# Logits groups inside gate/up jobs, PV behind the up half, and another order of loads in a fused attention and gated-MLP kernel

## The chip, the cores and the metric

The kernel runs on one core of a Trainium2 chip. The metric is device time in microseconds for one execution. The kernel was run three times before the change; the median is what the change is compared with. The core has five engines that run side by side, each with a strict program order of its own: TensorE (PE: matmuls and their weight loads), VectorE (DVE), ScalarE (ACT), GpSimd (POOL) and SyncE (SP), which here mostly issues transfers (DMA). An engine waits when an instruction at the head of its order needs something that another engine or a transfer hasn't finished.

## What is computed

One block of a transformer with adaptive layer norm on 2048 rows of 448 columns. `c` and `w_mod` give six modulation vectors (sa, ca, ga, sb, cb, gb). The attention half works in four segments of 512 rows with 16 heads of 28 columns: causal softmax attention inside a segment, mixed by a gate with a read-out of a memory `M` that sums what earlier segments left. The second half is a gated MLP with 1792 hidden columns. Cut to what matters:

```python
h = layernorm(x) * (1 + ca) + sa
q, k, v = h @ wq, h @ wk, h @ wv            # 16 heads, 4 segments of 512
for s in range(4):
    logits = einsum('bhqd,bhkd->bhqk', qs, ks) * scale + mask
    a_dot = softmax(logits) @ vs
    pq = phi(qs)                            # t + 1 where t > 0, else exp(t)
    a_mem = (pq @ M) / (pq @ z + 1e-6)
    outs.append(g * a_mem + (1 - g) * a_dot)
    M = M + phi(ks).T @ vs;  z = z + phi(ks).sum()
x = x + ga * (concat(outs) @ wo)
h = layernorm(x) * (1 + cb) + sb
x = x + gb * ((sigmoid(h @ w_gate) * (h @ w_up)) @ w_down)
```

## The kernel before

The program is written as a schedule by hand. Attention runs over 4 segments, 4 head chunks `hc` of four heads, and 3 groups of logits per chunk. After each group, `run_fill` takes jobs (projections, output projection, gate/up, down) from a queue `fill` to keep TensorE busy, as many as `pace` allows by a nominal cost in ns. `later` puts small steps off to a nominal time; `tick` moves that time on; `need` forces what is still put off. All small PSUM results come from four buffers in rotation (`m_f32`, `m_bf16`); a logits group takes the other four banks.

```python
def logits(s, hc, g):
    ...
    lg = ps_lg.tile([P, 4, 512], F32, tag="lg", name="lg")
    ...
            for hs in range(4):
                r = slice(HP * hs, HP * hs + Dh)        # four row tiles of 32 rows, side by side
                nc.tensor.matmul(lg[:, hs, wid:wid + nq], lhsT=kT[r, hc, kb * P:(kb + 1) * P],
                                 rhs=qT[r, hc, kb * P:L], start=True, stop=True, tile_position=(HP * hs, 0))
    ...
    nc.scalar.activation(pT[:, :, w0:w0 + wid], lg[:, :, 0:wid], AF.Exp, scale=scale)
    ...

def pv(s, hc):
    ...                                                 # 40 matmuls into acc
    if s > 0:
        mem = m_f32("mem")
        ...                                             # 4 matmuls: memory read-out
    ...
    # r1 = 1/(acc sums), t1 = acc * r1, r2 = 1/(mem sums), t2 = mem * r2, ou = t1 + t2, all on VectorE

def gate_up(s, f0):
    h = hT_of[("2", s)]
    fcs = (f0, f0 + 1)
    ...
    for g, f in zip(gp, fs):
        for k in range(3):                              # 128 rows
            nc.tensor.matmul(g[:, 0:L], lhsT=wg_sb[:, k, f], rhs=h[:, k, :], start=(k == 0), stop=False)
    ...
    for g, u, f in zip(gp, up, fs):
        for dst, r, first in ((g, 0, False), (u, LW, True)):   # the last 64 rows: a pair of 64-row tiles
            nc.tensor.matmul(dst[:, 0:L], lhsT=wgu_sb[r:r + LW, f], rhs=h[r:r + LW, 3, :], start=first,
                             stop=not first, tile_position=(r, 0))
        tt = work.tile([P, L], F32, tag="tt", bufs=3)
        nc.scalar.activation(tt[:], g[:, 0:L], AF.Tanh, scale=0.5)
        tts.append(tt)
    for fc, u, f, tt in zip(fcs, up, fs, tts):
        for k in range(3):                              # 128 rows
            nc.tensor.matmul(u[:, 0:L], lhsT=wu_sb[:, k, f], rhs=h[:, k, :], start=False, stop=(k == 2))
        ...
        nc.vector.scalar_tensor_tensor(ft[:], tt[:], 1.0, u[:, 0:L], op0=ALU.add, op1=ALU.mult)
```

The layer norm of a later segment is spread in nominal time: statistics, `norm_t` with a DMA transpose on SyncE, and `modulate`, which waits for that transpose:

```python
            for t in range(TPS):
                later(5200 + 500 * t, lambda t=t: ln.norm(t) if by_pe else ln.norm_t(t), tag)
            if not by_pe:
                for kc in range(NK):
                    later(14500 + 500 * kc, lambda kc=kc: ln.modulate(kc, 0), tag)
```

The start of the program: `pad_copy` brings wq and wk from a staging buffer into their padded form.

```python
    for k in range(NK):
        pad_copy(nc.scalar, wq_sb, wq_st, k)
    for t in range(TPS):
        ln0.norm(t)
        if t == 1:
            for k in range(NK):
                pad_copy(nc.vector, wk_sb, wk_st, k)
            mod_evac(((0, 0), (1, 1)))
        for kc in range(NK):
            nc.tensor.transpose(pts[kc][:, t * P:(t + 1) * P], ln0.xn[:, t, kc * P:(kc + 1) * P], ident[:])
    for kc in range(NK):
        ln0.pe_evac(pts[kc], kc, 0)
```

And the main loop:

```python
            for g in range(3):
                if prev[0] >= 0 and g == 1:
                    pv(*prev)
                    tick(1100)
                logits(s, hc, g)
                tick(450)
                ...                                     # at s >= 1, hc == 1: queue wo, down, gate/up jobs
                debt = run_fill(pace[0] + debt)
                ...
                if prev[0] >= 0 and g == 2:
                    otr(*prev)                          # DMA transpose of ou to oT
```

`prep_b1` makes the replicated row ga, loads w_mod's fourth column block and scales wo; `prep_b3`, put between the first gate/up jobs, makes the row gb and scales wd in seven steps. w_mod passes through two buffers, `wm[j]` in buffer `j % 2`.

Of the kernel before, what the change touches and what calls it, by code (L numbers as in the profile page):

```python
# [13 lines left out]
P = 128  # L14
# [3 lines left out]
def kernel(  # L18
# [86 lines left out]

    load_x(nc.sync, 0, 2)
    load_x(nc.scalar, 2, 4)
    nc.sync.dma_start(c_col[:], c.rearrange("o (k p) -> p (o k)", p=KP))
# [37 lines left out]
    load_w(nc.sync, wq_st, A_wq)  # L146
    load_w(nc.scalar, wk_st, A_wk)
# [84 lines left out]
    def mod_rep(j, mul, name):  # L232
        rp = m_f32("rp")
        for k in range(NK):
            nc.tensor.matmul(rp[:, 0:D], lhsT=silu_bc[:, k, :], rhs=wm[j][:, k * D:(k + 1) * D],
                             start=(k == 0), stop=(k == NK - 1))
        rep = const.tile([P, D], BF16, name=name, tag="rep")
        nc.scalar.mul(rep[:], rp[:, 0:D], mul)
        return rep
# [61 lines left out]
    def ln1_start(s, by_pe=False):  # L301
        def start():
            ln = ln1_of[s] = LN([x_sb[:, s * TPS + t, :] for t in range(TPS)], ("1", s))
            tag = ("ln1", s)
            for t in range(TPS):
                later(900 * t, lambda t=t: ln.stats(t), tag)
            later(3600, lambda: ln.rstd(0, TPS), tag)
            for t in range(TPS):
                later(5200 + 500 * t, lambda t=t: ln.norm(t) if by_pe else ln.norm_t(t), tag)
            if not by_pe:  # L310
                for kc in range(NK):
                    later(14500 + 500 * kc, lambda kc=kc: ln.modulate(kc, 0), tag)
        return (0, start)
# [43 lines left out]
    def phi(src, wait, tag, then=None):  # L357
        e = work.tile([P, L], BF16, tag="e", bufs=6, name="e")
        nc.scalar.activation(e[:], src, AF.Exp)

        def fin():
            r = work.tile([P, L], BF16, tag="r", bufs=2, name="r")
            nc.vector.tensor_scalar(r[:], src, 0.0, 1.0, op0=ALU.max, op1=ALU.add)
            nc.vector.tensor_tensor(e[:], e[:], r[:], ALU.min)
            if then:
                then(e)
        later(wait, fin, tag)
        return e
# [30 lines left out]
    def logits(s, hc, g):  # L399
# [16 lines left out]
        if g == 0 and s > 0:  # L416
            pq_of[u] = phi(qT[:, hc, :], 4500, ("pq", u))
# [8 lines left out]
    def pv(s, hc):  # L426
# [12 lines left out]
        if s > 0:  # L439
            mem = m_f32("mem")  # L440
            memv = mem[:].rearrange("p (t h e) -> p t h e", h=4, e=HP)
            need(("pq", u), ("rm", s))
            pq = pq_of.pop(u)
            for qb in range(TPS):
                nc.tensor.matmul(memv[:, qb, :, 0:ME], lhsT=pq[:, qb * P:(qb + 1) * P], rhs=rm_of[s][:, hc, :, :],
                                 start=True, stop=True)
        ou = ou_bufs[(s * NHC + hc) % 2]
        ou_of[u] = ou
        cb = lambda i: coef[:, i:i + 1, hc * 4:(hc + 1) * 4].to_broadcast([P, TPS, 4])
        r1 = work.tile([P, TPS, 4], F32, tag="r1", bufs=2)  # L450
        nc.vector.tensor_tensor(r1[:], accv[:, :, :, Dh], cb(0), ALU.mult)
        nc.vector.reciprocal(r1[:], r1[:])

        def bc(r):
            return r[:].rearrange("p t (h o) -> p (t h) o", o=1).to_broadcast([P, TPS * 4, Dh])

        def num(a):
            return a[:].rearrange("p (th e) -> p th e", e=HP)[:, :, 0:Dh]

        ouv = ou[:].rearrange("p t h e -> p (t h) e")[:, :, 0:Dh]  # L460
# [4 lines left out]
        nc.vector.tensor_tensor(t1[:], num(acc), bc(r1), ALU.mult)  # L465
        r2 = work.tile([P, TPS, 4], F32, tag="r2", bufs=2)
        nc.vector.scalar_tensor_tensor(r2[:], memv[:, :, :, Dh], 1e-6, cb(1), op0=ALU.add, op1=ALU.mult)
        nc.vector.reciprocal(r2[:], r2[:])
        t2 = work.tile([P, TPS * 4, Dh], F32, tag="t2", bufs=1)
        nc.vector.tensor_tensor(t2[:], num(mem), bc(r2), ALU.mult)  # L470
        nc.vector.tensor_tensor(ouv, t1[:], t2[:], ALU.add)
# [29 lines left out]

    def gate_up(s, f0):
# [9 lines left out]
        for g, u, f in zip(gp, up, fs):  # L512
            for dst, r, first in ((g, 0, False), (u, LW, True)):
                nc.tensor.matmul(dst[:, 0:L], lhsT=wgu_sb[r:r + LW, f], rhs=h[r:r + LW, 3, :], start=first,  # L514
                                 stop=not first, tile_position=(r, 0))
            tt = work.tile([P, L], F32, tag="tt", bufs=3)
            nc.scalar.activation(tt[:], g[:, 0:L], AF.Tanh, scale=0.5)  # L517
            tts.append(tt)
        for fc, u, f, tt in zip(fcs, up, fs, tts):
# [36 lines left out]
    def gu_jobs(s):  # L556
        return [(GU, lambda fc=fc: gate_up(s, fc)) for fc in range(0, NFC, 2)]
# [6 lines left out]
    def run_fill(ns):  # L564
        while fill and ns > 0:
# [6 lines left out]
    def prep_b1():  # L572
        ga = mod_rep(2, 1.0, "ga")
        wm[4] = load_wm(nc.sync, 4)
        for k in range(0, NK, 2):
# [6 lines left out]
    def prep_b2():  # L582
        mod_cols(((3, 2), (4, 3)))
        wm[5] = load_wm(nc.sync, 5)

    def prep_b3():
        gb = mod_rep(5, 0.5, "gb")
        for fc in range(0, NFC, 2):
            later(1700 * fc + 800, lambda fc=fc: scale_w(wd_sb, fc, gb), "wd")
# [15 lines left out]
    for t in range(TPS):  # L605
# [3 lines left out]
        if t == 1:  # L609
            silu_ops()  # L610
# [3 lines left out]
    for k in range(NK):  # L614
        pad_copy(nc.scalar, wq_sb, wq_st, k)
    for t in range(TPS):
        ln0.norm(t)
        if t == 1:
            for k in range(NK):
                pad_copy(nc.vector, wk_sb, wk_st, k)  # L620
            mod_evac(((0, 0), (1, 1)))
        for kc in range(NK):
            nc.tensor.transpose(pts[kc][:, t * P:(t + 1) * P], ln0.xn[:, t, kc * P:(kc + 1) * P], ident[:])
    for kc in range(NK):
        ln0.pe_evac(pts[kc], kc, 0)
    load_x(nc.sync, TPS, 2 * TPS)
# [16 lines left out]
    def load_wm3():  # L643
        wm[3] = load_wm(nc.sync, 3)
# [11 lines left out]
    def spread(jobs, steps, every):  # L656
        steps, res = list(steps), []
        for i, j in enumerate(jobs):
            res.append(j)
            if i % every == every - 1 and steps:  # L660
# [4 lines left out]
    early_loads = [load_wo, lambda: load_x(nc.sync, 3 * TPS, 4 * TPS), load_wm3] \  # L665
        + [piece(wg_sb, B_w_gate, k) for k in range(NK)] + [piece(wu_sb, B_w_up, k) for k in range(NK)]
    fill.extend(sp(load_bw2))
    fill.extend(spread(j0[3:6] + sp(late_consts) + j0[6:10] + [ln1_start(2)] + j0[10:] + ln1_pe_jobs(1) + m[0][0:1]
                       + j1[:8], early_loads, 2))
    fill.extend([ln1_start(3)] + m[1][0:1] + j1[8:] + [(1000, prep_b1)])  # L670
    fill.extend(spread(j2[:4] + m[0][1:] + j2[4:8] + [(2000, prep_b2)], [piece_wd(f, min(f + 4, NFC)) for f in range(0, NFC, 4)], 2))
    fill.extend(j2[8:] + m[1][1:])
    fill.extend(j3)
# [7 lines left out]
    for s in range(NSEG):  # L681
        for hc in range(NHC):
            prev = (s, hc - 1) if hc else (s - 1, NHC - 1)
            for g in range(3):
                if prev[0] >= 0 and g == 1:
                    pv(*prev)
                    tick(1100)
                logits(s, hc, g)
                tick(450)
                if s >= 1 and hc == 1 and g == 0:  # L690
# [3 lines left out]
                    fill.clear()  # L694
                    for w in wo_jobs(s - 1):
                        fill.append(w)
                        if tail and s > 1:
                            fill.append(tail.pop(0))
# [4 lines left out]
                    else:  # L703
                        fill.extend(h2_jobs(s - 1) + gj[:1] + [(1000, prep_b3)] + m[2][0:1] + gj[1:5] + m[2][1:] + gj[5:])
# [8 lines left out]
    dj = down_jobs(last - 1)  # L713
    run_fill(2000)
    pv(last, NHC - 1)
    tick(1100)
    run_fill(6000)
    otr(last, NHC - 1)
    fill.extend(dj[:2])
    run_fill(3000)  # L720
# [3 lines left out]
    fill.extend(dj[2:])  # L724
# [33 lines left out]
```

The softmax here doesn't subtract the row's maximum and nothing guards it: scores larger than these inputs give would overflow.

## Time and profile before

| what | value |
|---|---|
| device time, median of 3 runs | 274.89 us (274.32 to 276.37) |
| span of the profiled execution | 275.1 us |
| instructions | 5225 |
| mean granted TensorE clock | 0.975 |
| HBM read and written | 10.67 MB, 1.84 MB |

Some of the groups of instructions in that profile, with what their engine waited for before them:

| line, engine, what | count | busy us, mean ns | idle before, most of it ended by |
|---|---|---|---|
| L415 ScalarE exp of logits | 48 | 76.6, 1595 | 55.1, PE logits |
| L524 VectorE product of gate and up | 56 | 36.8, 684 | 36.7, PE up |
| L517 ScalarE tanh of the gate | 56 | 30.3, 595 | 44.9, PE gate |
| L530 PE down | 224 | 43.7, 353 | 0.0 |
| L509 PE gate, full array | 155 | 40.4, 380 | 1.0, VectorE |
| L521 PE up, full array | 164 | 40.2, 381 | 0.5 |
| L412 PE logits (four forms) | 256 | 17.7, 310 | 3.4, ScalarE exp |
| L437 PE PV | 640 | 19.0, 177 | 1.4, GpSimd mask |

A line number is that of the kernel before. Busy time of an engine counts its instructions from start to end; matmuls overlap, so a mean duration of 380 ns goes with a start every 216 ns. "Idle before" is what the engine stood still just ahead of such an instruction, and the name is that of the engine whose result ended the wait. A row of tenths shows one digit for each of 40 equal slices of the span; the clock row is the share of full clock that TensorE was granted. L274, L374 and L477 are the DMA transposes that SyncE issues (hT, pk, oT); L278 is `modulate`; L342 brings kT out of PSUM.

### The profile page before, as it was taken

To read this page: it belongs to the slowest core of one execution; us is meant where nothing else is said; L and a number is where in the kernel's file an instruction comes from. 1 tells how busy PE (TensorE), PEld (TensorE's weight loads), DVE (VectorE), ACT (ScalarE), POOL (GpSimd) and SP (SyncE) were. 2 spreads that over 40 slices of the span, in tenths; PEclk is the share of its full clock that TensorE was granted. 3 is DMA by queue.
4 is the path that set the end of the run, shared out by engine and by line. 5 is a ranking of instruction groups with operands and counts; after the bars stand their busy time and mean duration, and the time that the engine had idled before them with its cause. 6 is when DMAs were issued, how large, how long until landed. Compare 5 with 4: busy or idle time off the path is not lost.

```text
span 275.1 us, 5225 instructions
## 1 busy us (share of the span) xinstructions
PE 246.6 (90%) x2029; PEld 114.7 (42%) x2054; DVE 185.0 (67%) x429; ACT 139.2 (51%) x171; POOL 69.6 (25%) x130
## 2 busy tenths in 40 slices
PE   7599798896788689889989989999999999999995
PEld 2344444553343334444344443535443445433352
DVE  4569799944378748897995665797774669434421
ACT  1268489774727578666622767653564220033300
POOL 4109421450424312114351222224220004000000
PEclk9979799997979999999999999999999999999999
DMA  5999539488911100220031100003120001400001
GB/s 144 263 235 284 113 64 221 70 147 142 245 40 39 42 19 0 60 57 21 19 76 35 38 19 21 1 21 84 28 55 20 21 0 42 94 9 0 0 26 43
DMA packets 40960, 19.66 MB, mean 71 GB/s; under 512 B 29672, under 2 KB 40040, under 8 KB 40936
## 3 DMA queue, kind: packets, MB, share of 16 engines
q1 hardware_dynamic: 39720, 18.30, 30.8%
q10 hardware_dynamic: 1216, 1.03, 1.4%
q8 instruction: 16, 0.26, 0.5%
q14 instruction: 8, 0.07, 0.1%
HBM read 10.67 MB, written 1.84 MB: 45 GB/s over the span
## 4 chain that ended last, share of the span: by engine, by line
PE 44%; DVE 20%; DMA 6%; ACT 3%; issue 3%; SPq 1%; POOL 1%; DVEq 0%; ACTq 0%
PE ups L521 12%; PE dps L530 11%; PE gps L509 10%; PE gps L514 4%; DMA hT<-xn 3%; DVE st L257 3%; PE lg L412 2%; DVE x_sb L489 2%; PE acc L437 2%; DVE fT L524 2%; ACT pT L415 2%; DMA oT<-ou 2%; PE pwo L486 2%; DMA pk<-e 2%; DVE t L470 1%
## 5 line engine op out<-in xcount | busy, mean ns | idle before, releaser
L415 ACT ACTIVATE pT<-lg 128x2048 bf16<-128x2048 f32 (+1 forms) x48 | 76.6, 1595 | 55.1 <-PE lg L412 55.0
L524 DVE SCALAR_TENSOR_TENSOR fT<-tt,ups 128x512 bf16<-128x512 f32 x56 | 36.8, 684 | 36.7 <-PE ups L521 28.5
L423 POOL TENSOR_SCALAR_AFFINE_SELECT pT<-pT 128x512 bf16<-128x512 bf16 x64 | 41.2, 662 | 67.7 <-ACT pT L415 67.7
L517 ACT ACTIVATE tt<-gps 128x512 f32<-128x512 f32 x56 | 30.3, 595 | 44.9 <-PE gps L514 44.9
L530 PE MATMUL dps<-wd_sb,fT 128*128 128x448 bf16 x224 | 43.7, 353 | 0.0
L509 PE MATMUL gps<-hT,wg_sb 128*128 128x512 bf16 x155 | 40.4, 380 | 1.0 <-DVE t L465 0.4
L521 PE MATMUL ups<-hT,wu_sb 128*128 128x512 bf16 x164 | 40.2, 381 | 0.5 <-issue 0.5
L530 PEld LDWEIGHTS <-fT 128*128 128x128 bf16 x224 | 21.5, 98 | 20.5 <-issue 0.6
L521 PEld LDWEIGHTS <-wu_sb 128*128 128x128 bf16 x168 | 14.1, 98 | 25.5 <-issue 12.3
L261 POOL TENSOR_SCALAR rs<-mv 128x1 f32<-128x1 f32 (+2 forms) x21 | 5.2, 248 | 75.9 <-DVE mv L258 75.9
L509 PEld LDWEIGHTS <-wg_sb 128*128 128x128 bf16 x168 | 15.2, 98 | 20.0 <-issue 2.7
L437 PEld LDWEIGHTS <-pT 128*128 128x128 bf16 x640 | 18.8, 97 | 5.9 <-issue 2.2
L337 PE MATMUL pq<-hT,wq_sb 128*128 128x512 bf16 x60 | 18.2, 406 | 3.2 <-DVE hT L296 1.9
L257 DVE BATCH_NORM_STATS2 st<-x_sb 128x6 f32<-128x448 bf16 x32 | 19.8, 617 | 1.8 <-DMA x_sb<-in_A_x_dram 1.3
L412 PE MATMUL lg<-qT,kT 28*128 28x512 bf16 (+3 forms) x256 | 17.7, 310 | 3.4 <-ACT pT L415 3.4
L437 PE MATMUL acc<-vt,pT 128*128 128x29 bf16 x640 | 19.0, 177 | 1.4 <-POOL pT L423 1.2
L514 PE MATMUL ups<-hT,wgu_sb 64*128 64x512 bf16 x56 | 18.0, 382 | 2.0 <-DVE t L470 1.1
L534 DVE TENSOR_TENSOR ot<-dps,x_sb 128x448 bf16<-128x448 f32 x16 | 9.8, 618 | 13.2 <-PE dps L530 10.7
L514 PE MATMUL gps<-hT,wgu_sb 64*128 64x512 bf16 x56 | 17.1, 381 | 1.6 <-DVE hT L278 1.3
L349 PE MATMUL pv<-wv_sb,hT 128*128 128x448 bf16 x64 | 14.6, 367 | 4.2 <-DVE kT L342 4.2
L337 PE MATMUL pq<-hT,wk_sb 128*128 128x512 bf16 x61 | 17.0, 394 | 1.0 <-ACT qT L340 0.7
L486 PE MATMUL pwo<-wo_sb,oT 128*128 128x448 bf16 x64 | 14.8, 366 | 2.2 <-DMA oT<-ou 2.1
(88 smaller groups left out, 261.9 us busy)
## 6 DMA issues: line engine op xcount, KB each, us to landing
wm<-in_w_mod_dram SPq DMA_DIRECT2D x5, 392.0 KB, 7.9
out_dram<-ot SPq DMA_DIRECT2D x16, 112.0 KB, 1.7
x_sb<-in_A_x_dram SPq DMA_DIRECT2D x3, 448.0 KB, 7.3
wg_sb<-in_B_w_gate_dram SPq DMA_DIRECT2D x3, 448.0 KB, 9.1
wu_sb<-in_B_w_up_dram SPq DMA_DIRECT2D x3, 448.0 KB, 3.9
wd_sb<-in_B_w_down_dram SPq DMA_DIRECT2D x3, 448.0 KB, 3.7
wm<-in_w_mod_dram ACTq DMA_DIRECT2D x1, 392.0 KB
wo_sb<-in_A_wo_dram SPq DMA_DIRECT2D x4, 98.0 KB
```

Source lines behind the costliest of these rows:

```text
L257: nc.vector.bn_stats(st[:], self.srcs[i])
L337: nc.tensor.matmul(pq[:, 0:L], lhsT=head_cols(w_sb, k, hc), rhs=h[:, k, :], start=(k == 0), stop=(k == NK - 1))
L412: nc.tensor.matmul(lg[:, hs, wid:wid + nq], lhsT=kT[r, hc, kb * P:(kb + 1) * P], rhs=qT[r, hc, kb * P:L], start=True, stop=True, tile_posi ...
L415: nc.scalar.activation(pT[:, :, w0:w0 + wid], lg[:, :, 0:wid], AF.Exp, scale=scale)
L423: nc.gpsimd.affine_select(out=blk, in_=blk, compare_op=ALU.is_ge, fill=0.0, base=0, pattern=[[0, 4], [1, P]], channel_multiplier=-1)
L437: nc.tensor.matmul(accv[:, qb, hs, 0:ME], lhsT=pT[:, hs, c0:c0 + P], rhs=vt[:, kb, hc * 4 + hs, 0:ME], start=(kb == 0), stop=(kb == qb))
L509: nc.tensor.matmul(g[:, 0:L], lhsT=wg_sb[:, k, f], rhs=h[:, k, :], start=(k == 0), stop=False)
L514: nc.tensor.matmul(dst[:, 0:L], lhsT=wgu_sb[r:r + LW, f], rhs=h[r:r + LW, 3, :], start=first, stop=not first, tile_position=(r, 0))
L517: nc.scalar.activation(tt[:], g[:, 0:L], AF.Tanh, scale=0.5)
L521: nc.tensor.matmul(u[:, 0:L], lhsT=wu_sb[:, k, f], rhs=h[:, k, :], start=False, stop=(k == 2))
L524: nc.vector.scalar_tensor_tensor(ft[:], tt[:], 1.0, u[:, 0:L], op0=ALU.add, op1=ALU.mult)
L530: nc.tensor.matmul(dp[:, 0:D], lhsT=fT_of[(s, fc)][:, t * P:(t + 1) * P], rhs=wd_sb[:, fc, :], start=(fc == 0), stop=(fc == NFC - 1))
```

## The change

Some changes are of order only; no matmul is added or taken away.

- A gate/up job is split: the full-array gate matmuls and the 64-row tile pairs are a first job, the full-array up matmuls a second. `run_fill` stops behind a first half where it can, the next logits group comes right behind the tile pairs, and the up half follows it.
- PV of the chunk before comes behind that up half instead of ahead of the logits group.
- The memory read-out becomes a step of its own one group earlier (group 0 instead of 1), with t2 in two buffers.
- gb is made in `prep_b1`, and wd is scaled from there on instead of between the gate/up jobs; for that w_mod's blocks 3 and 5 change places in the order of loads, ga and gb get a buffer each, and wd is loaded before gate and up weights.
- At the start, c is loaded first on ScalarE's queue, wq and wk are each split over both queues, the norms and transposes of segment 0 come ahead of the copies, and the copies of wq are shared by ScalarE and VectorE.
- Segments 2 and 3 start their first norm at other places in the queue and modulate at other nominal times; the tail is queued in another way, and phi's buffers go from six to five.

```diff
+    nc.scalar.dma_start(c_col[:], c.rearrange("o (k p) -> p (o k)", p=KP))
     load_x(nc.sync, 0, 2)
     load_x(nc.scalar, 2, 4)
-    nc.sync.dma_start(c_col[:], c.rearrange("o (k p) -> p (o k)", p=KP))
...
-    load_w(nc.sync, wq_st, A_wq)
-    load_w(nc.scalar, wk_st, A_wk)
+    for st, w in ((wq_st, A_wq), (wk_st, A_wk)):
+        nc.sync.dma_start(st[:, 0:2, :], w[0:2 * P, :].rearrange("(k p) n -> p k n", p=P))
+        nc.scalar.dma_start(st[:, 2, :], w[2 * P:3 * P, :])
+        nc.scalar.dma_start(st[0:LW, 3, :], w[3 * P:D, :])
...
-                    later(14500 + 500 * kc, lambda kc=kc: ln.modulate(kc, 0), tag)
+                    later(mod_at + 500 * kc, lambda kc=kc: ln.modulate(kc, 0), tag)
...
-            pq_of[u] = phi(qT[:, hc, :], 4500, ("pq", u))
+            pq_of[u] = phi(qT[:, hc, :], 3600, ("pq", u))
...
+    def mem_read(s, hc):
+        u = (s, hc)
+        mem = m_f32("mem")
...
+        t2 = work.tile([P, TPS * 4, Dh], F32, tag="t2", bufs=2)
+        t2_of[u] = t2
         nc.vector.tensor_tensor(t2[:], num(mem), bc(r2), ALU.mult)
...
+        half[0] = (s, fcs, up, fs, tts)
+
+    def gate_up2():
+        s, fcs, up, fs, tts = half.pop(0)
+        h = hT_of[("2", s)]
         for fc, u, f, tt in zip(fcs, up, fs, tts):
...
-        return [(GU, lambda fc=fc: gate_up(s, fc)) for fc in range(0, NFC, 2)]
+            jobs += [(GU - 6 * MM, lambda fc=fc: gate_up(s, fc)), (6 * MM, gate_up2)]
...
-        while fill and ns > 0:
+        while fill and (ns > 0 or fn is gate_up2 and fill[0][0] == GU - 6 * MM):
...
     def prep_b1():
         ga = mod_rep(2, 1.0, "ga")
         wm[4] = load_wm(nc.sync, 4)
+        gb = mod_rep(5, 0.5, "gb")
+        wm[3] = load_wm(nc.sync, 3)
+        for fc in range(0, NFC, 2):
+            later(8000 + 2000 * fc, lambda fc=fc: scale_w(wd_sb, fc, gb), "wd")
...
-    for k in range(NK):
-        pad_copy(nc.scalar, wq_sb, wq_st, k)
     for t in range(TPS):
         ln0.norm(t)
         if t == 1:
-            for k in range(NK):
-                pad_copy(nc.vector, wk_sb, wk_st, k)
             mod_evac(((0, 0), (1, 1)))
...
+    for k in range(2):
+        pad_copy(nc.scalar, wq_sb, wq_st, k)
+        pad_copy(nc.vector, wq_sb, wq_st, 2 + k)
     for kc in range(NK):
         ln0.pe_evac(pts[kc], kc, 0)
+    for k in range(NK):
+        pad_copy(nc.vector, wk_sb, wk_st, k)
...
-    fill.extend([ln1_start(3)] + m[1][0:1] + j1[8:] + [(1000, prep_b1)])
...
+    fill.extend(j1[8:9] + [ln1_start(3, mod_at=19000)] + m[1][0:1] + j1[9:] + [(1800, prep_b1)])
+    fill.extend(spread(j2[:4] + m[0][1:] + j2[4:8] + [(2000, prep_b2)], early_loads[11:], 2))
+    fill.extend(j2[8:] + j3[:2] + m[1][1:] + j3[2:])
...
             for g in range(3):
+                logits(s, hc, g)
+                tick(450)
+                if fill and fill[0][1] is gate_up2:
+                    fill.popleft()[1]()
+                    tick(6 * MM)
+                    debt -= 6 * MM
+                if prev[0] > 0 and g == 0:
+                    mem_read(*prev)
+                    tick(250)
                 if prev[0] >= 0 and g == 1:
                     pv(*prev)
-                    tick(1100)
-                logits(s, hc, g)
-                tick(450)
+                    tick(1000)
...
-    run_fill(6000)
+    run_fill(1500)
     otr(last, NHC - 1)
-    fill.extend(dj[:2])
-    run_fill(3000)
+    run_fill(3500)
     for c, fn in wo_jobs(last):
         fn()
         tick(c)
-    fill.extend(dj[2:])
+    fill.extend(dj)
```

## The prediction, made before the changed kernel was run

> **What bounds the kernel now.** I read the page first (busy shares, the 40 slices), then the busy time by stage, then what TensorE (PE) waited for, then the chain that ended last. From the page:
>
> ```profile
> PE 246.6 (90%) x2029; PEld 114.7 (42%) x2054; DVE 185.0 (67%) x429; ACT 139.2 (51%) x171; POOL 69.6 (25%) x130
> PEclk9979799997979999999999999999999999999999
> ```
>
> TensorE is the bound, but not evenly, and its granted clock dips to 0.7 in four slices, all before 84 us. Busy time by stage (columns: stretch, length, then busy us and instructions for PE, weight loads, VectorE (DVE), ScalarE, GpSimd; then clock, DMA share, GB/s):
>
> ```profile
> 0.00:77.00 77.00, 63.00 (x563) 30.97 (x571) 51.51 (x137) 48.67 (x62) 27.32 (x53) 0.93 0.81 174
> 77.00:132.00 55.00, 47.66 (x466) 22.19 (x473) 44.14 (x105) 35.50 (x42) 16.08 (x28) 0.97 0.15 33
> 132.00:224.00 92.00, 88.51 (x764) 40.58 (x773) 65.19 (x142) 47.42 (x54) 22.94 (x41) 1.00 0.14 33
> 224.00:275.10 51.10, 47.39 (x240) 20.98 (x241) 24.15 (x48) 7.63 (x15) 3.31 (x8) 1.00 0.12 29
> ```
>
> PE idles 14.0 us in the first stage, 7.3 in the second, 3.5 in the third and 3.7 in the last, most of that after its last matmul. So the open money lies before 132 us; after it only fewer or cheaper PE steps help. PE's waits, longest in total (us, times, longest):
>
> ```profile
> PE pv L349 <- DVE kT L342: 4.2, 2, 2.8
> PE lg L412 <- ACT pT L415: 3.4, 6, 1.1
> PE cp L218 <- DMA wm<-in_w_mod_dram: 2.2, 1, 2.2
> PE pwo L486 <- DMA oT<-ou: 2.1, 1, 2.1
> PE pq L337 <- DVE hT L296: 1.9, 2, 1.6
> ```
>
> The largest is a wait for VectorE, and VectorE was itself waiting: its own waits list `DVE hT L278 <- DMA hT<-xn` with one wait of 5.1 us. The chain between 58 and 80 us (start, us, what) shows it:
>
> ```profile
> 59.20 1.26 SPq L274
> ...
> 60.55 2.46 DMA hT<-xn
> ...
> 63.13 0.73 DVE hT L278 x2
> 63.87 0.60 DVE kT L342
> 64.47 0.61 DVE hT L278 x2
> 65.08 4.28 DMA pk<-e
> ...
> 71.31 5.57 DMA oT<-ou
> ```
>
> The modulation of segment 3's hT stands too early in VectorE's strict order. Its transposed input lands only at 63 us, the kT evacuation behind it is held, PSUM stays full and PE stops until 64.5. The steady state, PE's timeline:
>
> ```profile
> 158.50 0.29 PE L412 MATMUL lg<-qT,kT 28*128 28x256 bf16 x4
> 158.72 1.47 PE L509 MATMUL gps<-hT,wg_sb 128*128 128x512 bf16 x6
> 160.12 0.39 PE L514 MATMUL gps<-hT,wgu_sb 64*128 64x512 bf16 x1
> ...
> 160.66 1.47 PE L521 MATMUL ups<-hT,wu_sb 128*128 128x512 bf16 x6
> 162.06 0.40 PE L412 MATMUL lg<-qT,kT 28*128 28x512 bf16 x4
> 162.39 1.17 PE L437 MATMUL acc<-vt,pT 128*128 128x29 bf16 x40
> ```
>
> Start to start, six full matmuls take 1.40 us before the tile pairs. The two pairs 160.12 and 160.35 are 0.23 apart, and the full matmuls follow 0.31 after the second pair. Plain spacing is 0.216 (the chain has six gps matmuls in 1.29 us from 241.80), so six should take 1.30: each passage between a full-array matmul and a row-tiled one costs about 0.10 us. The same shows at logits: 0.33 from 162.06 to the next full matmul, for one 512-wide step.
>
> **What the skill says.** The Trainium skill, "TensorEngine Tiling (Array Packing)", section "Tiling Modes" (Key Properties), says that changing the tiling mode, not merely the tile, drains TensorE. The 0.10 us agrees with a drain at 128-to-64, 64-to-128 and 128-to-32 rows; no matmul pair in this trace goes from 64 to 32 directly, so whether that passage costs the same isn't shown. "TensorE: Matmul & The Clock Gate", Part 1, says an idle window of about 3.4 us puts the clock to half. The trace agrees in effect, after waits of even 2.8 us: four pv matmuls from 64.52 took 1.65 us against 0.93 for four at 23.43, and the stretch 60 to 68 us has a clock of 0.79. "DMA: Bandwidth & Descriptors", section "Issuing engines are not separate DMA queues", says that loads issued from two engines run on the same 16 DMA engines and interleave. So the split of wq and wk brings order (wq whole before wk), not bandwidth. Here they landed nearly together: VectorE's wk copies began at 11.87 us and ScalarE's wq copies at 12.34, and DMA was 0.93 busy over the first 20 us.
>
> **The change part by part.**
>
> *Start.* Before, VectorE holds the last two norms behind the wk copies (DMA wait of 2.4 us to 11.87), so the transposes end about 14.1; ScalarE does four wq copies (2.0 us) before its two hT evacuations (14.27 to 15.72). The first q matmul starts at 14.77. After, the norms go first, so transposes can end about 12.5, right after the modulation columns (wm lands 10.54, columns out about 11.6). The wq copies are two of 0.56 us on ScalarE beside two of about 0.27 on VectorE (the means of such copies before), and wk's come after the evacuations. If wq lands about 11.5, the first q matmul can start near 13.2. Minus 1.5 us; the c vector first on its queue also frees silu, which held VectorE until 7.4.
>
> *Segment 2 and 3 normalisation.* Segment 2's starts two jobs (1.5 us) earlier with modulation 0.5 us closer: it meets the two hT waits of PE at 47 to 49 us (0.23 + 0.68): minus 0.9. For segment 3 the modulation moves from 14.5 to 19 us after a start that is one job later. The 2.8 us stall goes, and with it the half-clock work after it (4 pv matmuls 1.65 for 0.93, PV, logits and dM some 0.5 more): gross about 4. Against it, hT, pk and oT transposes still queue behind one another on SyncE, which issues one per 1.2 us, and the new second wm load sits among them. I keep half: minus 2.
>
> *oT wait.* PV of (0,3) ran late because of that stall, and its transpose took 5.57 us behind three wd loads. It should come some 3 us earlier, and two segment-3 projections now stand ahead of dM. Minus 1 of the 2.1 us wait.
>
> *wd scaling.* Seven VectorE multiplies of 0.63 us (4.4 us) leave 100 to 128 us, where VectorE is 90% busy (12.64 of 14 us between 104 and 118) and is the chain, for roughly 52 to 80 us, where it has room before 77. PE idles 4.8 us between 95 and 132. The memory read-out one group ahead takes r2, its reciprocal and t2 (1.0 us) out of the burst after PV, and its PSUM buffer is released earlier (waits of PE on t L470: 1.1 us in all). Together minus 3.0: 2.5 in that stretch and 0.5 before it.
>
> *Logits behind tile pairs.* Walking the fill queue with the job costs in the code, 14 of the 48 logits groups come directly behind a gate half and ahead of its up half. There 128-64-128 plus 128-32-128 (four passages) becomes 128-64-32-128 (three): 14 x 0.10 = minus 1.4. The tanh now precedes the exp on ScalarE, so up results no longer wait behind a 1.88 us exp (VectorE waited 8.2 us for tt): minus 0.7 of the 2.9 us that PE waits between 132 and 224.
>
> *PV later, the tail, the rest.* PV (40 matmuls, 1.0 us) only moves. In the tail the same queue walk gives the same order of gate, wo and down jobs as before; zero. The matmul count is unchanged.
>
> Sum: 1.5 + 0.9 + 2 + 1 + 3.0 + 1.4 + 0.7 = 10.5 us, giving 264.4. I do not take it all. PE is one in-order engine fed by transposes whose pace is set elsewhere, so an early gain can be waited away at the next landing: I strike 3 of the 5.4 us won before 77 us, which leaves **267.4**.
>
> **Rivals.** (a) *The transpose queue is the bound until 77 us.* The segment-1 pk transposes need the buffer that dM of segment 0 frees at 53.4, and everything on SyncE stands behind them; DMA share is 0.81. Then the removed kT stall becomes a wait at dM or pwo, and only the later parts count (5.1 us): about 270. For it: the chain passes from hT to pk to oT without PE. Against it: PV, which starts the last oT, was itself late through the stall. (b) *A new wait for w_mod.* Both remaining wm loads (392 KB each) are now issued after the second replicated row, near 53 us, and the modulation columns of the second norm need both; they ran at 58.5, with the one load issued at 54.65. If the second lands 2 us late PE stalls there, about 269.5. (c) *PSUM.* Between gate half and up half all four small buffers are held; if PV or read-out then makes the next gate half wait for fT, 14 jobs at 0.2 us give back 3 us: about 270. The order (read-out and PV after the up half) speaks against it. (d) *64 to 32 costs double*: then the name-giving part brings nothing, 268.8.
>
> **Range and chances.** The parts are independent enough that one rival at a time is likely: 267 to 270; several together, 272 to 273. If early gains carry through, 263. The 2% line is 269.4, two microseconds above my figure, so I give faster 0.62, same 0.34. A loss over 2% needs new waits larger than all the gains; nothing points there: 0.04.
>
> **What would show it.** Right: first q matmul near 13.2; no 2.8 us PE wait on kT and no VectorE wait of 5 us on hT; fewer clock dips between 60 and 84; no wd multiply after 100 us; logits starting about 0.10 behind a 64-row pair's last matmul with the up half 0.10 behind them; PE busy above 92% of the span. Wrong: a long PE wait on wm, pk or oT before 77 us; tile-to-tile gaps of 0.2 us; waits on fT or acc at gate halves; or a start no earlier because wq still lands at 12.3.

## The result and the profile after

The changed kernel took 267.94 us (median of 4 runs, 267.26 to 268.67), the kernel before beside it 275.63. The ratio is 0.9726 (95% interval 0.967 to 0.9782); on another chip, with more runs, it was 0.9748 (0.9718 to 0.9778). The prediction was 267.4.

The sum was close; how it came about was not all as predicted. From the page after (the same two lines as of before):

```profile
PE 241.1 (91%) x2030; PEld 113.3 (43%) x2054; DVE 183.4 (69%) x431; ACT 137.8 (52%) x169; POOL 70.8 (27%) x130
PEclk9999999988999999999999999999999999999999
```

The four dips of the clock to 0.7 are gone, two to 0.8 are left. Busy time by stage, cut at the same times as before:

```profile
0.00:77.00 77.00, 64.97 (x627) 31.93 (x635) 58.19 (x155) 49.81 (x62) 28.51 (x57) 0.98 0.78 174
77.00:132.00 55.00, 49.58 (x494) 23.81 (x498) 45.73 (x109) 38.17 (x45) 20.21 (x35) 1.00 0.17 37
132.00:224.00 92.00, 88.57 (x722) 41.24 (x728) 64.03 (x142) 42.21 (x50) 22.10 (x40) 1.00 0.14 33
224.00:275.10 51.10, 37.99 (x193) 16.36 (x193) 15.50 (x28) 7.60 (x14) 0.01 (x1) 0.99 0.09 24
```

In the first 77 us TensorE (PE) is busy for 2.0 us more and starts 64 more matmuls: the clock, not only idle time, was won there. PE's waits after (us in total, times, longest; in this kernel L339 are the q and k projections, L351 v, L387 the memory sum dM, L494 the output projection, L220 the modulation columns, and L344 brings kT out of PSUM):

```profile
PE lg L414 <- ACT pT L417: 2.8, 5, 0.8
PE pq L339 <- DVE hT L298: 2.8, 2, 2.3
PE pv L351 <- DVE kT L344: 2.0, 2, 1.1
PE pwo L494 <- DMA oT<-ou: 1.9, 1, 1.9
PE dM L387 <- DMA pk<-e: 1.6, 1, 1.6
PE ups L524 <- DVE x_sb L497: 1.5, 2, 0.8
PE warm L613 <- POOL ident L160: 1.4, 1, 1.4
PE cp L220 <- DVE silu L183: 1.2, 1, 1.2
PE cp L220 <- DMA wm<-in_w_mod_dram: 1.1, 1, 1.1
...
PE acc L439 <- ACT tt L527: 0.5, 1, 0.5
PE mem L463 <- ACT tt L527: 0.5, 1, 0.5
```

The 2.8 us stall on kT is gone. In its place stand waits for the landing of w_mod (1.1) and of pk (1.6), and the wait for oT is almost as long as it was (1.9 of 2.1; 1.4 in a second profile of this kernel). Two waits on tanh near the end are new: PV and read-out of the last chunk stand between a gate half and its up half.

Cut by what PE does instead of by time, the gain lies elsewhere than predicted. Starts in us from PE's timeline in each profile, of the first q matmul, the first dM, the first gate matmul, the first down matmul and the last segment's output projection, and the span:

| kernel | first q | first dM | first gate | first down | last wo | span |
|---|---|---|---|---|---|---|
| before | 14.77 | 52.38 | 93.45 | 135.80 | 224.36 | 275.1 |
| changed | 12.54 | 48.90 | 90.06 | 127.23 | 215.34 | 265.7 |
| difference, stage by stage | -2.2 | -1.2 | +0.1 | -5.2 | -0.5 | -0.4 |

The second replicated row (two rows' eight matmuls take 1.68 us, so 0.8 for one) moved from the fourth of these stages into the second; apart from it the second won 2.1 us and the fourth 4.3, and the third, where the stall was, nothing. The profiled execution of before was one of its longer ones (276.8 us), so the two traces differ by 9.4 us where the medians differ by 7.7.

### The profile page after: what moved, and what is told of

It reads as the page before. It is cut to its first block, busy times and chain, and to the rows that moved or that the text cites. A ratio compares the mean times of both kernels' runs of the same rounds, so it can differ in the third digit from the quotient of the medians.

```text
span 265.7 us, 5242 instructions
## 1 busy us (share of the span) xinstructions
PE 241.1 (91%) x2030; PEld 113.3 (43%) x2054; DVE 183.4 (69%) x431; ACT 137.8 (52%) x169; POOL 70.8 (27%) x130
## 4 chain that ended last, share of the span: by engine, by line
PE 43%; DVE 6%; ACT 2%; issue 2%; DMA 1%; POOL 0%; DVEq 0%
PE dps L545 14%; PE ups L536 10%; PE gps L519 9%; PE gps L524 4%; PE acc L439 2%; PE pwo L494 2%; DVE fT L539 1%; PE lg L414 1%; ACT pT L417 1%; DVE ot L549 1%; DMA hT<-xn 1%; ACT tt L527 1%; DVE t L451 1%; DVE hT L280 1%; PE mem L463 1%
## 5 line engine op out<-in xcount | busy, mean ns | idle before, releaser
L425 POOL TENSOR_SCALAR_AFFINE_SELECT pT<-pT 128x512 bf16<-128x512 bf16 x64 | 42.6, 681 | 68.9 <-ACT pT L417 68.9
L519 PE MATMUL gps<-hT,wg_sb 128*128 128x512 bf16 x154 | 39.8, 379 | 0.8 <-issue 0.2
L519 PEld LDWEIGHTS <-wg_sb 128*128 128x128 bf16 x168 | 15.9, 98 | 17.7
L339 PE MATMUL pq<-hT,wq_sb 128*128 128x512 bf16 x60 | 16.8, 379 | 3.4 <-DVE hT L298 2.8
L439 PEld LDWEIGHTS <-pT 128*128 128x128 bf16 x640 | 17.5, 96 | 4.3 <-issue 2.9
L267 DVE TENSOR_SCALAR xn<-x_sb,mv,rs 128x448 bf16<-128x448 bf16 x32 | 16.0, 519 | 4.6 <-POOL rs L264 4.6
L339 PE MATMUL pq<-hT,wk_sb 128*128 128x512 bf16 x61 | 16.3, 380 | 0.9 <-ACT qT L342 0.5
L351 PE MATMUL pv<-wv_sb,hT 128*128 128x448 bf16 x64 | 15.1, 380 | 2.0 <-DVE kT L344 2.0
```

What stands on the lines that cost most here:

```text
L339: nc.tensor.matmul(pq[:, 0:L], lhsT=head_cols(w_sb, k, hc), rhs=h[:, k, :], start=(k == 0), stop=(k == NK - 1))
L425: nc.gpsimd.affine_select(out=blk, in_=blk, compare_op=ALU.is_ge, fill=0.0, base=0, pattern=[[0, 4], [1, P]], channel_multiplier=-1)
L439: nc.tensor.matmul(accv[:, qb, hs, 0:ME], lhsT=pT[:, hs, c0:c0 + P], rhs=vt[:, kb, hc * 4 + hs, 0:ME], start=(kb == 0), stop=(kb == qb))
```

## Experiments

The rows that the experiments add to that table (the changed kernel was run again as their partner):

| kernel | first q | first dM | first gate | first down | last wo | span | ratio to before (95%) |
|---|---|---|---|---|---|---|---|
| changed, again | 12.63 | 49.10 | 89.91 | 127.08 | 215.21 | 265.5 | 0.9748 (0.9718 to 0.9778) |
| nosplit | 12.55 | 50.66 | 91.60 | 131.18 | 219.26 | 269.6 | 0.9873 (0.9844 to 0.9902) |
| up1 | 12.45 | 49.69 | 90.77 | 128.26 | 216.42 | 267.6 | 0.9772 (0.974 to 0.9805) |
| memlate | 12.52 | 48.88 | 89.95 | 129.12 | 218.81 | 269.8 | 0.9901 (0.9863 to 0.9939) |
| b_mem | 13.47 | 51.35 | 92.99 | 134.08 | 223.25 | 274.1 | 0.9998 (0.9969 to 1.0026) |
| wdlate | 12.65 | 49.02 | 89.50 | 127.87 | 215.99 | 266.6 | 0.9801 (0.9778 to 0.9824) |
| mod145 | 12.65 | 50.01 | 90.85 | 128.02 | 216.13 | 266.4 | 0.9789 (0.9768 to 0.981) |
| nostart | 14.44 | 53.17 | 94.09 | 131.25 | 219.36 | 270.0 | 0.9865 (0.9845 to 0.9885) |
| nostart_warm | 14.08 | 51.71 | 92.27 | 129.43 | 217.55 | 267.8 | 0.981 (0.9775 to 0.9844) |
| b_start | 12.63 | 50.03 | 90.23 | 132.39 | 220.97 | 271.4 | 0.992 (0.9885 to 0.9955) |
| tuned1 | 13.15 | 48.76 | 89.35 | 126.52 | 213.53 | 263.8 | 0.969 (0.9652 to 0.9728) |
| tuned2 | 12.54 | 48.82 | 87.80 | 124.95 | 211.94 | 262.6 | 0.9556 (0.9517 to 0.9596) |

The second run of the changed kernel, up1, memlate and tuned1 ran on one chip, the others on another. So differences between two kernels below are those of their ratios to the kernel before on the same chip, times 275 us, with both intervals combined as root of squares.

The partner run:

> The changed kernel itself, on the same chip as the next three, to measure their differences against. All theories: 267 to 269, ratio to before 0.970 to 0.980.

Measured 267.95 us, 0.9748. It is the reference for all that follows.

### The split undone

```diff
-            jobs += [(GU - 6 * MM, lambda fc=fc: gate_up(s, fc)), (6 * MM, gate_up2)]
+            jobs += [(0, lambda: None), (GU, lambda fc=fc: (gate_up(s, fc), gate_up2()))]
```

> The changed kernel with one thing undone: gate/up jobs whole again, so no logits group stands between a gate half and its up half; PV and memory read-out still come behind the logits group. My theory (14 row-tile passages of 0.10 us saved, little else, and the split also makes PE wait for tanh in the tail): 1 to 1.5 us slower than the changed kernel, about 269.3, ratio to before 0.977. Rival A (the split also pays by putting tanh ahead of the exp on ScalarE): 3 us or more slower, 271 and above, with PE waits on tt between 95 and 224 us. Rival B (what the passages save is waited away): no slower than 268.2.

Measured 271.41 us: 3.4 us slower (plus or minus 1.1). Of the trace's 4.1 us, 1.7 were lost before the first gate job, where the two programs are the same; the mean clock of that execution was 0.981 against 0.994. From the first gate to the last wo it is 2.4 us. So the split pays more than its passages, as rival A said, but by another path than tanh: no PE wait on tanh is found in this run. PE's timeline of it:

```profile
109.27 0.40 PE L414 MATMUL lg<-qT,kT 28*128 28x512 bf16 x4
109.59 0.39 PE L463 MATMUL mem<-rm,e 128*128 128x116 bf16 x4
111.70 0.40 PE L414 MATMUL lg<-qT,kT 28*128 28x384 bf16 x8 [1.72 <-ACT pT L417]
```

A whole gate/up job (nominal 3.2 us) overdraws the pace of 2.3 us per group, so the next group gets no job and stands right behind the one before it, waiting for its exp to free the logits banks. Waits of this kind add up to 5.7 us here, 2.8 in the changed kernel. In the changed kernel there is an up half between any two such groups:

```profile
101.88 0.29 PE L414 MATMUL lg<-qT,kT 28*128 28x256 bf16 x4
102.10 1.47 PE L536 MATMUL ups<-hT,wu_sb 128*128 128x512 bf16 x6
103.41 1.46 PE L519 MATMUL gps<-hT,wg_sb 128*128 128x512 bf16 x6
104.80 0.39 PE L524 MATMUL gps<-hT,wgu_sb 64*128 64x512 bf16 x1
...
105.03 0.38 PE L524 MATMUL gps<-hT,wgu_sb 64*128 64x512 bf16 x1
...
105.34 0.40 PE L414 MATMUL lg<-qT,kT 28*128 28x512 bf16 x4
```

The same lines show the passages: from the second pair (105.03) to the logits 0.31 us, that is 0.216 and 0.10. The way from 64-row to 32-row tiles costs what any passage costs, so three are paid for four.

### One up matmul ahead of the logits

```diff
+        nc.tensor.matmul(up[0][:, 0:L], lhsT=wu_sb[:, 0, fs[0]], rhs=h[:, 0, :], start=False, stop=False)
         half[0] = (s, fcs, up, fs, tts)
...
-            for k in range(3):
+            for k in range(1 if u is up[0] else 0, 3):
```

> The changed kernel with one of the six up matmuls of each gate/up job moved ahead of the logits group, so that the passage from 64-row to 32-row tiles becomes 64 to 128 to 32, while each logits group keeps its half-job neighbours (five of the six up matmuls). It separates the two ways in which the split can pay. If it pays by saved passages of the array: 14 x 0.10 = 1.4 us slower than the changed kernel, and if that is most of the 4 us which the unsplit kernel lost, 3 us or more. If it pays by what stands between two logits groups (no group right behind another, waiting for its exp): the passages cost 1.4 us and the rest stays won, so 1 to 1.7 us slower. If passages cost nothing at the end: within 0.5 us.

Measured 268.69 us: 0.7 us slower (plus or minus 1.2), which is no difference that the interval can hold. In the trace the way from first gate to last wo is 125.65 us against 125.28 and 125.30 in the two profiles of the changed kernel. Thirteen passages more should be 1.3 us. But the waits of logits on exp on this way are 0.7 us shorter (1.36 instead of 2.06): a passage ahead of such a wait costs nothing at the end. And in the tail the moved matmul fills part of the two waits on tanh: from the last PV inside the main loop to the last wo it is 19.83 us instead of 20.12. 1.3 less 0.7 less 0.3 is about the 0.35 seen. So the saved passages are worth less than their 1.3 us, and the larger part of the split's worth is what stands between the groups: up1, which keeps that and gives up the passages, is 2.8 us (plus or minus 1.2) faster than nosplit, 2.0 us by the traces.

### The memory read-out put back

```diff
-                if prev[0] > 0 and g == 0:
+                if prev[0] > 0 and g == 1:
                     mem_read(*prev)
```

> The changed kernel with the memory read-out moved back by one logits group, directly ahead of PV. Theory (the read-out ahead spreads VectorE's burst and frees a PSUM buffer early): 1 to 2 us slower than the changed kernel, with more PE waits on VectorE's t and x_sb between 95 and 224 us. Rival (VectorE isn't the bound there any more): within 0.5 us; and the tail loses one PE wait of 0.5 us for tanh (read-out between two halves).

Measured 271.68 us: 4.2 us slower (plus or minus 1.3), the largest effect of a part taken out, and more than twice my theory's 1 to 2. PE's longest waits in this run include:

```profile
PE gps L519 <- DVE t L470: 1.9, 3, 1.0
```

A gate matmul doesn't read t2; it waits for the PSUM buffer that t2's multiplication was the last to read. PV and read-out together take two of the four small buffers and give them back only after one burst on VectorE. The loss is 2.0 us between first gate and first down and 1.6 from there to the last wo. The three waits shown are about half of it; the rest wasn't taken apart.

The reverse is the early read-out alone in the kernel before:

```diff
-        if s > 0:                      # in pv: four matmuls into mem, and further down r2 and t2
-            mem = m_f32("mem")
...
+        nc.vector.tensor_tensor(ouv, t1[:], t2_of.pop(u)[:], ALU.add)
+    def mem_read(s, hc):               # as in the changed kernel, t2 in two buffers
...
                 logits(s, hc, g)
                 tick(450)
+                if prev[0] > 0 and g == 0:
+                    mem_read(*prev)
+                    tick(250)
```

> The kernel before with only the memory read-out one logits group ahead (phi's minimum correspondingly at nominal 3600 instead of 4500). Putting it back in the changed kernel cost 3.7 us. If the early read-out pays by itself (two of the four small PSUM buffers no longer wait for one burst on VectorE): 272 or less, ratio 0.990. If it pays only because PV stands behind the logits group in the changed kernel: within 1 us of before.

Measured 275.42 us, ratio 0.9998 (two of its 14 runs, at a lower clock, are not in the ratio): nothing, within 0.8 us, so the second theory held. First gate to first down takes 41.1 us instead of 42.4, but the whole is no shorter. As I read it, in the kernel before a logits group lies between PV and the next gate job, while in the changed one a gate half, which asks for four buffers, can follow PV at once: the early read-out makes PV's new place affordable and isn't a gain of its own. That reading is argued from the order of the code, not shown by a run.

### wd scaled late again

```diff
-            later(8000 + 2000 * fc, lambda fc=fc: scale_w(wd_sb, fc, gb), "wd")
+            later(41400 + 1700 * fc, lambda fc=fc: scale_w(wd_sb, fc, gb), "wd")
```

> The changed kernel with the seven wd multiplies on VectorE put off to where they stood before (between the gate/up jobs, some 100 to 128 us); gb is still made early. Theory (VectorE was the chain there; the move was worth 2.5 us): 270.5, with PE waits on VectorE between 95 and 132 us up by some 2 us. Rival (with the memory read-out one group ahead and the logits split, VectorE has room there): within 0.7 us of the changed kernel.

Measured 269.19 us: 1.5 us slower (plus or minus 1.0); by the trace 1.2 us from first gate to first down, against 37.17 in the changed kernel. Between theory (2.5) and rival (0.7): VectorE does the same 4.4 us of multiplies there, from 93.8 to 116 us, and most of them no longer lengthen the whole. That early read-out and halves made the room is argued.

### Segment 3 modulated early again

```diff
-    fill.extend(j1[8:9] + [ln1_start(3, mod_at=19000)] + m[1][0:1] + j1[9:] + [(1800, prep_b1)])
+    fill.extend(j1[8:9] + [ln1_start(3, mod_at=14500)] + m[1][0:1] + j1[9:] + [(1800, prep_b1)])
```

> The changed kernel with the modulation of segment 3 back at nominal 14.5 us after the start of its norm, instead of 19. Theory (it stands in VectorE's order ahead of the kT evacuation and stops PE): the PE wait of pv on kT near 60 us comes back with 2 to 3 us, and 1.5 to 2.5 us of it stay at the end, about 270. Rival (the landing of pk and oT transposes sets the pace there anyway): the wait comes back but the waits on pk and oT shrink by as much, and the time stays within 0.7 us of 268.

Measured 268.92 us: 1.1 us slower (plus or minus 1.0). PE's longest waits include:

```profile
PE acc L439 <- DVE kT L344: 2.4, 1, 2.4
```

The stall is back, and the waits on pk (1.6) and oT (1.9) are gone from the list for that stage; the wait for w_mod stays (1.2). In the trace this exchange is even: from first dM to first gate it is 40.84 us, in the two profiles of the changed kernel 41.16 and 40.81. What this trace loses, it loses before the first dM, where the order of work is still the same: behind the same 2.3 us wait near 26 us its clock was 0.81 from 26 to 35 us, against 1.00 in both profiles of the changed kernel. So the stall of 2.8 us in the kernel before hid landings that come when they come; taking it away uncovered them. By the trace the rival was right for all of it; how much of the 1.1 us belongs to the modulation isn't shown.

### The old start

```diff
-    nc.scalar.dma_start(c_col[:], c.rearrange("o (k p) -> p (o k)", p=KP))
     load_x(nc.sync, 0, 2)
     load_x(nc.scalar, 2, 4)
+    nc.sync.dma_start(c_col[:], c.rearrange("o (k p) -> p (o k)", p=KP))
...                                    # whole wq on SyncE's queue, whole wk on ScalarE's; copies and norms as before
```

> The changed kernel with the start as before: c second on SyncE's queue, wq and wk whole on one queue each, wk copies ahead of the last two norms. Theory (the 2.2 us that the first q matmul came earlier carry through to the end): 270.1, ratio 0.981. Rival (the transpose queue sets the pace until 77 us and the lead is waited away there): within 0.7 us of the changed kernel, 268.0 to 268.7, with shorter PE waits on pk and oT before 77 us.

Measured 271.01 us: 3.2 us slower (plus or minus 1.0), though the first q matmul starts only 1.9 us later. By the first dM the lead lost is 4.1 to 4.3 us in the traces. One reason stands in the busy time by stage; the stretch from 12 to 20 us, first with the old start, then in the changed kernel:

```profile
12.00:20.00 8.00, 7.13 (x31) 3.30 (x32) 4.81 (x14) 4.38 (x9) 0.00 (x0) 0.58 1.13 263
```

```profile
12.00:20.00 8.00, 7.04 (x41) 2.77 (x40) 6.75 (x18) 5.69 (x7) 1.83 (x3) 1.00 1.00 246
```

With the old start PE idles in this run between 7.7 and 14.4 us except for the modulation columns, transposes and one dummy matmul, and the first projections run at about half clock (four q matmuls take 1.86 us, later 1.03). From 26 to 35 us the clock is lower too (0.86 against 1.00), as it was in mod145 with the new start. To part clock from lead, dummy matmuls were put into those gaps, their results unused:

```diff
-    NWARM, EARLY, KEEP = (20, 2), 2400.0, (0, 2, 2, 4)
+    NWARM, EARLY, KEEP = (29, 4), 2400.0, (0, 2, 2, 4)
```

> The changed kernel with the old start, as run already (ratio 0.9865), and 11 more dummy matmuls on TensorE before the first real work, so that its idle stretches between 8.3 and 14 us are filled. They compute nothing that is used. If about half of what the new start won is the granted clock (0.58 between 12 and 20 us with the old start, 1.00 with the new): the first q matmul stays near 14.4 us, the clock there rises to near 1, and the time falls by 1.5 to 2 us, ratio 0.980. If it is the lead alone: no faster than 0.9865.

Measured 269.81 us, ratio 0.981: 1.5 us faster than the same kernel without them (plus or minus 1.1), with the first q matmul at 14.08 and this clock:

```profile
12.00:20.00 8.00, 6.77 (x44) 3.09 (x42) 5.92 (x18) 6.16 (x10) 0.14 (x1) 1.00 1.13 266
```

So by the medians about half of the 3.2 us of the new start is the clock, with an interval from 0.4 to 2.6. The start doesn't settle the clock by itself: from 12 to 20 us three executions with the old start had 0.58 (nostart), 0.79 (before) and 1.00 (b_mem), and with the new start nosplit had 0.79. And the new start alone, put into the kernel before (the edit of nostart the other way round):

> The kernel before with only the new start (loads of c, wq and wk, norms ahead of copies, copies shared). Taking it out of the changed kernel cost 3.8 us in ratio to before. If it is worth the same alone: 271.0, ratio 0.986, and no half clock between 12 and 20 us. If the kernel before loses the lead again at the stalls that it still has (kT near 62 us, oT at 76): 273.5, ratio 0.995.

Measured 273.14 us, ratio 0.992: 2.2 us (plus or minus 1.0), between the two. The kT stall (2.8) and the oT wait (1.4 instead of 2.1) are still there. At the first gate this run is level with the changed kernel (90.23), which by then has made one row more (0.8); what it lacks comes after (42.2 us to the first down, as before).

### Going on from the result

Three moves, each against a wait in the list of after:

```diff
-    fill.extend(spread(j0[3:6] + sp(late_consts) + j0[6:8] + [ln1_start(2, mod_at=14000)] + j0[8:] + ln1_pe_jobs(1) + m[0][0:1]
+    fill.extend(spread(j0[3:6] + sp(late_consts) + j0[6:8] + j0[8:] + ln1_pe_jobs(1) + [ln1_start(2, mod_at=12000)] + m[0][0:1]
...
+    drain()                            # runs a waiting up half
     mem_read(last, NHC - 1)
-    run_fill(2000)
+    run_fill(1900)
+    drain()
     pv(last, NHC - 1)
...                                    # tanh of c ahead of the last wq load on ScalarE's queue
```

> The changed kernel with three further moves: statistics of segment 2 behind the transposes of segment 1 in VectorE's order (against the PE wait of 2.3 us near 26 us and the half clock behind it), tanh of c ahead of the later loads on ScalarE's queue (against the PE wait of 1.2 us on silu near 9 us), and the last read-out and PV behind an up half instead of between two halves (against two PE waits of 0.5 us on tanh near 203 us). If they all carry through: 3.5 to 4.5 us faster than the changed kernel, 264. If the transposes' pace until 77 us takes back the first two: 267.

Measured 266.18 us: 1.6 us faster (plus or minus 1.3), less than half of the hope. From first down to last wo it took 87.0 us against 88.1: the tail's waits on tanh did cost 1.1 us. The rest won 0.6 by the first gate: the 2.3 us wait near 26 us went, but 1.2 on hT, 0.8 and 0.5 on kT and 0.9 on ou came in the same stage, and the tanh, moved ahead of a wq load, delayed the first q matmul to 13.15.

The next step went for the transposes. SyncE's timeline in the changed kernel has the two lines

```profile
42.87 8.25 SPq L376 DMA_TRANSPOSE pk<-e  x2
51.18 1.10 SPq L117 DMA_DIRECT2D wm<-in_w_mod_dram  x2
```

8.25 us for two transposes that take 1.2 each to issue: the second waits for the only pk buffer, which dM frees at 49.9, and all later transposes and w_mod stand behind it.

```diff
-            pk_of[s] = pipe.tile([P, NHC, TPS, P], BF16, tag="pk", bufs=1, name="pk")
+            pk_of[s] = pipe.tile([P, NHC, TPS, P], BF16, tag="pk", bufs=2, name="pk")
...                                    # fT buffers 16 -> 14, tt 3 -> 2; tanh of c one load later
```

> The first tuned version with two buffers for the transposed keys of the memory (pk) instead of one, paid for with two fT and one tt buffer less, and tanh of c one load later on ScalarE's queue. With one buffer SyncE stood still from 42.9 to 50 us ahead of the transposes of segment 1. If that wait set the pace until 77 us: the PE waits on pk (1.9) and oT (1.6) shrink by 2 us or more, 263.5 to 264.5. If the landing under load sets it: 266, as the first tuned version.

Measured 263.51 us, ratio 0.9556: 5.3 us faster than the changed kernel (plus or minus 1.3), 3.7 (plus or minus 1.5) faster than the first tuned version, and the best here. SyncE's timeline of this run:

```profile
45.25 2.52 SPq L377 DMA_TRANSPOSE pk<-e  x2
47.86 2.55 SPq L118 DMA_DIRECT2D wm<-in_w_mod_dram  x2
```

The first tuned version issues the same two transposes from 45.19, but they take until 50.98, and its w_mod loads come at 51.04. PE's wait for w_mod ahead of the second norm's modulation columns (0.3 in that version) is gone, the wait on pk is 0.9 instead of 1.9, on oT 1.5 instead of 1.6, and the first gate comes at 87.80 instead of 89.35. At the first dM the two tuned versions are level (48.82 and 48.76), though the later tanh lets the first q start at 12.54 instead of 13.15: the clock from 12 to 20 us was 0.84 in this execution and 1.00 in the other. The 1.6 us won by the first gate come after the first dM. So the pace of SyncE's transposes until 77 us was set by a buffer, at least in part; of the 2 us and more expected from pk and oT, 1.1 came. The smaller pools of fT and tt and the later tanh are in the same run and were not tried alone.

## Why the prediction was right, and which steps were not

*Start.* Right in mechanism and too small: 2.2 us earlier instead of 1.5, worth 3.2 at the end when taken out, 2.2 when put in alone. The missing term is the clock, as far as the runs tell. I read the half clock in the trace, as the Trainium skill's "TensorE: Matmul & The Clock Gate" (Part 1) has it for idle windows of about 3.4 us (here it came behind shorter waits, of 2.2 us before and 2.4 in nostart), but left it out of this step's sum; nostart_warm puts it at 1.5 us (plus or minus 1.1). A detail was wrong: c first on ScalarE's queue didn't free silu early. The fifth to seventh loads on that queue were issued at 4.75, 6.14 and 7.33 us and the tanh behind them ran at 9.13, later than before (6.81).

*Segment 2 and 3.* The stall went and the two short hT waits went. VectorE still waits for segment 3's input (4.0 us, to 62.06, where it was 5.1), but no PE wait on kT follows there any more. "I keep half: minus 2" was 1.1 by the medians of mod145 and nothing in its own stage of the trace: what PE no longer waits for kT, it waits for pk and oT. For segment 2 I hadn't seen that an earlier start puts four statistics ahead of segment 1's evacuation: that wait grew from 1.6 to 2.3 us.

*oT wait, minus 1.* Wrong: 1.9 of 2.1 us stayed (1.4 in the second profile), and 1.6 for pk came new (1.4). Waits on w_mod, pk and oT before 77 us were the sign that I had named for being wrong, and they came, 4.6 us in all. What I had as rival (a), the transpose queue as the pace, and rival (b), the wait for w_mod (1.1), both came true in part, so striking something for them was right; 3 of 5.4 us was a guess. The lead at the first gate is 3.4 us, or 4.2 with the moved row, against the 2.4 and 0.5 predicted for what lies ahead of the gate jobs.

*wd and read-out, minus 3.0.* The bundle was mis-sized by its smaller member. wd alone is 1.5, not most of it; undoing the early read-out costs 4.2. Yet alone it gives nothing: as I read it, it is tied to PV's new place, which I had put down as "only moves".

*Logits behind tile pairs, minus 1.4, and 0.7.* The passages are as predicted, 0.10 us each, 64 to 32 rows too; that answers rival (d). In the trace 13 groups, not 14, stand so: I had counted the last group of segment 3, which has PV ahead of it. What they are worth at the end is less than the 1.4 that I counted: giving them up again cost 0.7 us (plus or minus 1.2), 0.35 by the trace, since some stand ahead of a wait on exp. The further term was not tanh (VectorE's waits on it did fall from 8.2 to 3.5 us, but no PE wait of nosplit ends on it); it was the half-size job that separates two logits groups: 2.0 of the 2.4 us that the trace of nosplit lost behind the first gate.

*The tail, zero.* Wrong by 1.0: the order of jobs is the same, but the halves put PV and read-out where all four PSUM buffers are held. That is rival (c), in two places instead of fourteen. It is also why the 88 us from first down to last wo won only 0.5 of the 1.4 that I expected of them (seven of the fourteen passages and 0.7 for tanh).

PE is busy 91% of the span, not above 92 as I had named for a sign of being right. So the total came right by errors of both signs, which is luck in the figure: too little for clock, read-out and spacing, too much for oT, the modulation, the passages and the last third. The parts taken out one at a time add up to 13 us, more than the 7 that were won, so single effects here can't be added. As I read it, start, stall and landings share the same stretch, and early read-out, halves and PV's place lean on one another.

## What to carry to other kernels

When an in-order engine is fed by jobs of uneven size, look at what stands between two steps that share one buffer; halving a job can pay more by filling that gap than by what it saves itself. Before removing a stall, look for the landings that it hides, and at which buffer sets their pace: the version with a second pk buffer ran 3.7 us faster than the one that had only moved work around. A gap in front of dense matmuls can cost more than its own length where a low clock follows it, as from 12 to 20 us in nostart (0.58); look at the clock of several executions before counting on it.

## What the runs showed of the hardware that was not expected

Going straight from 64-row to 32-row tiles costs about 0.10 us, as any other change of tiles here does (0.31 us from the second pair to the logits, where 0.216 is plain spacing). The same program gets a different clock from one execution to the next: four runs of the changed kernel with mean clocks of 0.994, 0.994, 0.987 and 0.981 took 267.26, 267.37, 268.51 and 268.67 us, so the scatter of 1.4 us goes with the clock here; but two later runs of the same kernel at 0.994 and 0.986 both took 267.23. Behind one and the same PE wait of 2.3 us near 26 us, the clock from 26 to 35 us was 1.00 in both profiles of the changed kernel and 0.81 in mod145. And a load issue can hold back computation on its engine: on ScalarE's queue four loads were issued from 0.78 to 2.31 us and the fifth only at 4.75; why the fifth waited wasn't tried.
